# Attention and two expert layers on one core: first scores ahead of first transposes, and an opening spread over three units

## Chip, core and metric

One core of a Trainium2 chip runs the whole program. The metric is device time in microseconds. TensorE multiplies and transposes, VectorE (DVE), ScalarE (ACT) and GpSimd (POOL) do the element work, and SyncE (SP) issues most transfers.

## What is computed

Attention over 2 batches, 8 heads, 768 rows and a head dimension of 64, masked so that a query sees only the keys of its own hash bucket, then a gated layer, then a layer of 8 experts. The change touches only attention.

```python
mask = q_bucket[:, :, :, None] == k_bucket[:, :, None, :]
scores = scale * np.matmul(q, k.transpose(0, 1, 3, 2))
scores = np.where(mask, scores, -1000000000.0)
scores = scores - np.max(scores, axis=-1, keepdims=True)
attn = np.exp(scores)
attn = attn / (np.sum(attn, axis=-1, keepdims=True) + 1e-09)
return np.matmul(attn, v).astype(np.float32)
```

The bucket of a row is made of the signs of six projections. Here the mask is added to the scores by a second product over signed features, so that rows of other buckets fall to a large negative value.

## The kernel before

The program is under a manual schedule: every engine takes its instructions in the order in which the code emits them, and each waits for what it reads and for the tile that it overwrites.

Two heads make a pair, and there are eight pairs. A **unit** is one head and 256 query rows, so a pair has six units and attention has 48. One iteration `u` of the loop at L418 works on several units at once: scores of unit u, the turned probabilities of unit w = u-2, products with the values of x = u-3, and the end of y = u-4.

- `scores(u, t)` (L236): four products into one of two score tiles (`st`), for 128 query rows.
- `rowmax` (L251) on DVE and `expo` (L256) on ACT; `expo` is the last reader of a score tile and also gives the row sums. `masked` (L265) makes two small factors on POOL.
- `recip` (L274) on DVE and `normal` (L278) on POOL: the reciprocal of the sums, then two passes (L282) over the probability tiles of a unit.
- `etrans(w, m)` (L284), m = 0, 1, 2: four transposes into one of three tiles of the pool `ps_t`. `ehigh` (L298) copies the high part out on ACT, `elow` (L302) the low part on DVE; `elow` is the last reader of the tile.
- `pv` (L306): four products of one part with the values, twelve in a unit; `epilogue` (L321) copies out on ACT, and `finish` (L334) adds on POOL.
- A pair's queries and keys are turned ahead of time in six chunks (L346), one in each iteration: four of three transposes (`prep_t`, L154, with a high part on ACT and a low part on DVE) and two of six feature products (`prep_z`, L201). `stack_parts` (L181) and `stack_features` (L195) then copy the parts into the operand tile `p` by transfers from SP, and `load` (L128) fetches the next raw queries, keys and values on SP. `split_v` (L146) splits the values on POOL.

In an iteration TensorE gets scores(u,0), the chunk, etrans(w,1), scores(u,1), pv(x,0), etrans(w,2), pv(x,1), pv(x,2), and at the end etrans(u-1,0), whose copies (`ehigh(w, 0)`, `elow(w, 0)`) come in the next iteration. Weight preparation for the later layers is spread over the iterations by `hook(u, place)`.

The first head has no chunks ahead of it. `stacked` (L375) splits raw queries or keys in place with ACT and DVE, `turned` (L381) transposes them into `p`, and `featured` (L390) makes the mask's rows. L407 to L415 do the keys and the first half of the queries. In iteration 0 (L429 to L433, L454 to L465) the second head's queries, the second half of the first head's queries, the second head's keys and their transfers follow, with the loads of two values; its feature products come in iteration 1. The second pair's first two chunks are at the end of iteration 0 (L493).

Of the kernel before, what the change touches and what calls it, by code (L numbers as in the profile page):

```python
# [8 lines left out]
F32 = mybir.dt.float32  # L9
# [16 lines left out]
class Kernel:  # L26
# [84 lines left out]
    def attention(self, xh, xl, pools, hook):  # L111
        nc = self.nc
        sb, ps_s, ps_t, ps_pv = pools
        NB = self.proj.shape[1]
        NF = self.NF
        S, D = self.S, self.D
        NC = S // 128
# [8 lines left out]
        raw, HL, FT, P, VS, Z = {}, {}, {}, {}, {}, {}  # L126

        def load(i, which="qkv", queue=nc.sync):  # L128
            b, hp = pairs[i]
            for nm in which:  # L130
                src = {"q": self.q, "k": self.k, "v": self.v}[nm]
                if nm == "v":
                    t = sb.tile([128, 2, NC, D], F32, tag="raw", name="raw", bufs=4)
                else:
                    t = sb.tile([128, NC, 2, D], F32, tag="raw", name="raw", bufs=4)
                for j in range(2):
                    queue.dma_start(
                        out=t[:, j] if nm == "v" else t[:, :, j, :],
                        in_=src[b, 2 * hp + j].rearrange("(p c) d -> p c d", c=NC),
                    )  # L140
                raw[i, nm] = t
# [12 lines left out]
        def prep_t(i, nm, half):  # L154
            if half == 0:
                HL[i, nm] = sb.tile([128, 2, S], F32R, tag="hl" + nm, name="hl" + nm, bufs=2 if nm == "q" else 1)
            h, l = (0, 1) if nm == "q" else (1, 0)
            r, hl = raw[i, nm], HL[i, nm]
            pt = ps_t.tile([128, 512], F32, tag="t", name="pt")
            for m in range(3):  # L160
                c = 3 * half + m
                nc.tensor.transpose(pt[:, m * 128:(m + 1) * 128], r[:, c].rearrange("p h d -> p (h d)"), self.ident)
            cols = slice(384 * half, 384 * half + 384)
            scale = float(D) ** -0.5 if nm == "q" else 1.0

            def high():
                nc.scalar.mul(hl[:, h, cols], pt[:, :384], scale)

            def low():
                nc.vector.scalar_tensor_tensor(  # L170
                    hl[:, l, cols], pt[:, :384], scale, f32(hl[:, h, cols]), ALU.mult, ALU.subtract
                )

            return high, low
# [6 lines left out]
        def stack_parts(i, j, which="qk"):  # L181
            if which[0] == "q":
                P[i, j] = sb.tile([128, 4, S], F32R, tag="p", name="p", bufs=2)
            d = slice(64 * j, 64 * j + 64)
            p = P[i, j]
            if "q" in which:
                qs = f32(HL[i, "q"])
                nc.sync.dma_start(out=f32(p[0:64, 0:4:2]), in_=qs[d, 0:1].to_broadcast([64, 2, S]))
                nc.sync.dma_start(out=f32(p[64:128, 0]), in_=qs[d, 1])
            if "k" in which:  # L190
                ks = f32(HL[i, "k"])
                nc.sync.dma_start(out=f32(p[0:64, 1:4:2]), in_=ks[d])
                nc.sync.dma_start(out=f32(p[64:128, 1]), in_=ks[d, 1])
# [42 lines left out]
        def scores(u, t):  # L236
            i, j, g = units[u]
            c = 2 * g + t
            st = ST[u, t] = ps_s.tile([128, 2, 512], F32, tag="s", name="st")
            ql = slice(c * 128, (c + 1) * 128)  # L240
            p = P[i, j]
            for n in range(2):
                kl = slice(n * 384, (n + 1) * 384)
                nc.tensor.matmul(st[:, n, :384], p[:, 0, ql], p[:, 1, kl], start=True, stop=False)  # L244
                nc.tensor.matmul(st[:, n, :384], p[:KP, 2, ql], p[:KP, 3, kl], start=False, stop=True)  # L245
# [38 lines left out]
        def etrans(u, m):  # L284
            pt = ps_t.tile([128, 512], F32, tag="t", name="et")
            for t in range(2):
                for cc in range(2):
                    e = E[u, t].rearrange("p a b -> p (a b)")
                    c = 2 * m + cc
                    nc.tensor.transpose(  # L290
                        pt[:, (2 * cc + t) * 128:(2 * cc + t + 1) * 128],
                        e[:, c * 128:(c + 1) * 128], self.ident,
                    )
            eh = sb.tile([128, 512], F32R, tag="eh", name="eh", bufs=5)
            el = sb.tile([128, 512], F32R, tag="el", name="el", bufs=5)
            ET[u, m] = (eh, el, pt)
# [47 lines left out]
        NU = len(units)  # L344
# [3 lines left out]
        def chunk(n):  # L348

            i, m = divmod(n + 1, per)  # L350
            if i + 1 < len(pairs):
                f, *args = chunks[m]
                return f(i + 1, *args)
            return None

        raw[0, "k"], raw[0, "q"] = (sb.tile([128, NC, 2, D], F32, tag="raw", name="raw", bufs=4) for _ in range(2))
        for j in range(2):
            for nm, src, queue in (("k", self.k, nc.sync), ("q", self.q, nc.scalar)):
                queue.dma_start(
# [15 lines left out]
        def stacked(t, cs):  # L375
            s, r = stacks[t], raw[0, "qk"[t]][:, cs, 0, :]
            scale = 1.0 if t else float(D) ** -0.5
            nc.scalar.mul(s[:, cs, t, :], r, scale)
            nc.vector.scalar_tensor_tensor(s[:, cs, 1 - t, :], r, scale, f32(s[:, cs, t, :]), ALU.mult, ALU.subtract)
# [34 lines left out]
        self.features()  # L414
        load(1, "qk")  # L415

        opening = [[(nm, half) for half in range(2)] for nm in "qk"]
        for u in range(NU + 4):  # L418
            i, r = divmod(u, per)
            w, x, y = u - 2, u - 3, u - 4  # L420
            act, last, tr, out = u < NU, 0 <= u - 1 < NU, 0 <= w < NU, 0 <= x < NU
            if act:
                scores(u, 0)
            if y >= 0:
                epilogue(y)
            prep = chunk(u) if 0 < u < NU else None
            if act:
                rowmax(u, 0)
            if u == 0:  # L429
                for args in opening[0]:  # L430
                    for g in prep_t(0, *args):
                        g()
                stack_parts(0, 1, "q")  # L433
            if last:
                recip(u - 1)
            if tr:
                ehigh(w, 0)
            if last:
                normal(u - 1)
            hook(u, 3)  # L440
            if tr:
                elow(w, 0)
            hook(u, 0)
            if tr:
                etrans(w, 1)
                ehigh(w, 1)
            if act:
                scores(u, 1)
            if tr:
                elow(w, 1)  # L450
            if act:
                rowmax(u, 1)
                masked(u)
            if u == 0:  # L454

                stacked(0, slice(3, NC))
                turned(0, 1)
                featured(0, 1)
                for args in opening[1]:
                    for g in prep_t(0, *args):  # L460
                        g()
                stack_parts(0, 1, "k")
                load(0, "v")
                load(1, "v")
                hook(-1, 1)  # L465
            if u == 1:
                for half in range(2):
                    prep_z(0, half)[1]()
                stack_features(0, 1)
            if out:  # L470
                pv(x, 0)
            if act:
                expo(u, 0)
            if tr:
                etrans(w, 2)
            if out:
                pv(x, 1)
                pv(x, 2)
            if prep:
                prep[0]()  # L480
            hook(u, 2)
            if u in (1, 2):
                split_v(0, u - 1)
            if r >= 4 and i + 1 < len(pairs):
                split_v(i + 1, r - 4)
            if prep:
                prep[1]()
            if tr:
                ehigh(w, 2)
            if y >= 0:  # L490
                finish(y)
            hook(u, 1)
            if u == 0:  # L493
                for n in (-1, 0):
                    for g in chunk(n):
                        g()
            if r == 3 and i + 2 < len(pairs):
                load(i + 2)
            elif r >= 4 and i + 1 < len(pairs):
                stack(i + 1, r - 4)  # L500
            if last:
                etrans(u - 1, 0)
            if act:
                expo(u, 1)
            if tr:
                elow(w, 2)
            hook(u, 4)
# [876 lines left out]
```

## Time and profile before

| | us |
|---|---|
| median of 3 runs | 776.56 (776.48 to 777.78) |
| the profiled execution | 777.34 |
| its span, first to last instruction | 775.5 |
| TensorE busy | 755.2 (97%) |
| DVE, ACT, POOL busy | 494.3, 413.7, 485.4 |

The profiled execution is one run; its span leaves out 1.84 us before and after the instructions. In the rows below a line such as L290 is the line of the kernel that issued the instruction, PE is TensorE's products, PEld its weight loads, and names such as `et<-ident,e` say which tile is written from which. TensorE's busy time is modelled, since products overlap, so the start of one instruction to the start of a later one tells more than busy time.

### The profile page before, as it was taken

How to read it: one execution, taken by the hardware profiler on the slowest of the kernel's cores; microseconds unless marked ns; L12 is line 12 of the kernel's file. 1: busy time of each engine (PE TensorE's matmuls, PEld its weight loads, DVE VectorE, ACT ScalarE, POOL GpSimd, SP SyncE). 2: the span in 40 equal slices, each digit the busy share in tenths (PEclk: the TensorE clock that was granted, in tenths of full speed). 3: DMA queues.
4: the chain of work that ended last, by engine and by line, in shares of the span. 5: the costliest groups of instructions: out<-in, count | busy, mean ns of one | idle time of the engine just before them, and what ended most of it. 6: DMA issues, size and time to landing. Idle time of an engine off the chain costs nothing. (4 is left out here: it accounts for less than half of the span.)

```text
span 775.5 us, 13205 instructions
## 1 busy us (share of the span) xinstructions
PE 755.2 (97%) x4772; PEld 699.0 (90%) x4772; DVE 494.3 (64%) x790; ACT 413.7 (53%) x802; POOL 485.4 (63%) x530
## 2 busy tenths in 40 slices
PE   7999999999999999999999999999999999999996
PEld 5898899999999999999999999999998898899995
DVE  6898889988887755474664645533753755555551
ACT  3798898998988733321221212133443655565651
POOL 2689988888888767264553654644331865565651
PEclk9999999999999999999999999999999999999999
DMA  7864745844451313031111221063361666676620
GB/s 166 193 138 99 180 112 116 177 98 103 102 114 40 109 31 133 1 108 55 55 55 55 69 94 54 2 218 108 95 192 52 206 217 222 223 242 203 212 75 22
DMA packets 65443, 92.06 MB, mean 119 GB/s; under 512 B 28779, under 2 KB 32875, under 8 KB 65376
## 3 DMA queue, kind: packets, MB, share of 16 engines
q1 hardware_dynamic: 61168, 83.45, 38.7%
q0 software_dynamic: 2560, 7.34, 2.5%
q8 instruction: 39, 0.64, 0.3%
q10 hardware_dynamic: 1648, 0.39, 0.2%
q14 instruction: 28, 0.23, 0.1%
HBM read 66.08 MB, written 7.34 MB: 95 GB/s over the span
## 5 line engine op out<-in xcount | busy, mean ns | idle before, releaser
L658 PE MATMUL ab<-xh,w 128*128 128x384 f32 x768 | 204.0, 338 | 0.0
L658 PEld LDWEIGHTS ab<-xh,w 128*128 128x128 f32 x768 | 139.5, 188 | 0.8
L658 PE MATMUL ab<-xl,w 128*128 128x384 f32 x384 | 129.1, 336 | 0.0
L672 POOL TENSOR_TENSOR g<-a,g 128x384 fp32r<-128x384 f32 x48 | 52.4, 1092 | 101.0 <-ACT g L671 94.6
L907 POOL TENSOR_TENSOR w<-raw,w 128x1024 fp32r<-128x1024 f32 x36 | 87.5, 2432 | 37.3 <-ACT w L906 36.2
L254 DVE TENSOR_REDUCE nm<-st 128x1 f32<-128x768 f32 x96 | 91.3, 951 | 21.9 <-PE st L245 17.0
L304 DVE TENSOR_TENSOR el<-et,eh 128x512 fp32r<-128x512 f32 x144 | 96.0, 679 | 11.4 <-ACT eh L300 11.0
L684 PE MATMUL yp<-w,g 128*128 128x512 f32 x432 | 102.9, 390 | 0.0
L282 POOL TENSOR_SCALAR e<-e,s,mc 128x768 f32<-128x768 f32 x96 | 94.8, 995 | 5.2
L290 PE MATMUL et<-ident,e 128*128 128x128 f32 x576 | 91.5, 277 | 6.2 <-POOL e L282 3.7
L684 PEld LDWEIGHTS yp<-w,g 128*128 128x128 f32 x432 | 80.4, 188 | 14.9
L300 ACT CAST eh<-et 128x512 fp32r<-128x512 f32 x144 | 83.1, 587 | 18.6 <-PE et L290 16.3
L260 ACT ACTIVATE e<-st,nm 128x768 f32<-128x768 f32 x96 | 86.8, 904 | 5.2 <-DVE nm L254 2.2
L671 ACT CAST g<-a 128x384 fp32r<-128x384 f32 x48 | 24.7, 515 | 108.9 <-DVE a L670 108.9
L1001 PE MATMUL op<-w,hth 128*128 128x512 f32 x256 | 81.7, 400 | 0.0
L290 PEld LDWEIGHTS et<-ident,e 128*128 128x128 f32 x576 | 65.6, 140 | 16.7 <-POOL e L282 7.9
L951 PE MATMUL hp<-xgh,w 128*128 128x256 f32 x448 | 80.7, 281 | 0.0
L316 PE MATMUL pv<-eh,splv 128*128 128x256 f32 x288 | 76.9, 296 | 0.0
L666 ACT COPY a<-ab 128x384 f32<-128x384 f32 x48 | 22.9, 477 | 97.0 <-PE ab L658 95.5
L244 PE MATMUL st<-p 128*128 128x384 f32 x192 | 73.0, 380 | 0.4 <-ACT e L260 0.3
L907 DVE TENSOR_TENSOR w<-raw,w 128x1024 fp32r<-128x1024 f32 x28 | 63.0, 2251 | 16.1 <-ACT w L906 16.1
L658 PEld LDWEIGHTS ab<-xl,w 128*128 128x128 f32 x384 | 72.3, 188 | 0.8
(193 smaller groups left out, 1551.4 us busy)
## 6 DMA issues: line engine op xcount, KB each, us to landing
raw<-in_moe_w_dram SPq DMA_DIRECT2D x32, 1024.0 KB
p<-hlq SPq DMA_DIRECT2D x15, 384.0 KB
p<-hlk SPq DMA_DIRECT2D x15, 384.0 KB
raw<-in_moe_w_a_dram SPq DMA_DIRECT2D x5, 1024.0 KB
raw<-in_moe_w_b_dram SPq DMA_DIRECT2D x5, 1024.0 KB
raw<-in_moe_w_out_dram SPq DMA_DIRECT2D x5, 1024.0 KB
raw<-in_k_dram SPq DMA_DIRECT2D x16, 192.0 KB
raw<-in_v_dram SPq DMA_DIRECT2D x16, 192.0 KB
```

Of the source, the lines that this page charges most:

```text
L254: nc.vector.tensor_reduce(NM[u][:, t:t + 1], ST[u, t][:, :, :384], axis=AX.XY, op=ALU.max, negate=True)
L260: nc.scalar.activation(e, ST.pop((u, t))[:, :, :384], AF.Exp, bias=NM[u][:, t:t + 1], accum_out=SU[u][:, t:t + 1])
L282: nc.gpsimd.tensor_scalar(E[u, t], E[u, t], r[:, t:t + 1], c[:, t:t + 1], ALU.mult, ALU.add)
L290: nc.tensor.transpose(pt[:, (2 * cc + t) * 128:(2 * cc + t + 1) * 128], e[:, c * 128:(c + 1) * 128], self.ident,)
L300: nc.scalar.copy(eh, pt)
L304: nc.vector.tensor_tensor(el, pt, f32(eh), ALU.subtract)
L316: nc.tensor.matmul(p, w, parts[x][:, cc * 256:(cc + 1) * 256], start=(c == 0 and x == 0), stop=(c == NC - 1 and x == 1),)
L658: nc.tensor.matmul(p[:, :384], w[:, k, fs], x[:, k, cols], start=(k == 0 and n == 0), stop=(k == self.KD - 1 and n == 2),)
L684: nc.tensor.matmul(p, g[:, f, rows], w[:, f], start=(n == 0), stop=(n == 5))
L907: eng.tensor_tensor(l, raw, f32(h), ALU.subtract)
L951: nc.tensor.matmul(p[:, :256], w[:, k, fs], x[:, k], start=(n == 0), stop=(n == 3 * self.KD - 1))
L1001: nc.tensor.matmul(p, h[:, 2 * n + f, rows], w[:, f], start=(n == 0 and f == 0 and m == 0), stop=(n == 3 and f == 1 and m == 2),)
```

## The change

The raw tiles of the first queries and keys are made in the other order. In every iteration the first transposes now follow the scores: `etrans(w, 0)` at the start of iteration u, behind `scores(u, 0)`, in place of `etrans(u - 1, 0)` at the end of the iteration before. In iteration 0 the second half of the query stack is split ahead of the query transposes, the load of the first values follows the query transfers, and `expo(0, 0)` goes ahead of `turned` and `featured`. The second head's key transposes, key transfers and the load of the next values move to iteration 1. The second pair's first two chunks move to the end of iteration 1; its third and fourth are both in iteration 2. `hook(-1, 1)` holds no job. `masked` is not moved.

```diff
-        raw[0, "k"], raw[0, "q"] = (sb.tile([128, NC, 2, D], F32, tag="raw", name="raw", bufs=4) for _ in range(2))
+        raw[0, "q"], raw[0, "k"] = (sb.tile([128, NC, 2, D], F32, tag="raw", name="raw", bufs=4) for _ in range(2))
...
+        OPEN = {1: (), 2: (1, 2)}
...
             if act:
                 scores(u, 0)
+            if tr:
+                etrans(w, 0)
             if y >= 0:
                 epilogue(y)
-            prep = chunk(u) if 0 < u < NU else None
+            preps = [chunk(n) for n in OPEN.get(u, (u,))] if 0 < u < NU else []
+            preps = [prep for prep in preps if prep]
             if act:
                 rowmax(u, 0)
             if u == 0:
+                stacked(0, slice(3, NC))
                 for args in opening[0]:
                     for g in prep_t(0, *args):
                         g()
                 stack_parts(0, 1, "q")
+                load(0, "v")
+            if u == 1:
+                for args in opening[1]:
+                    for g in prep_t(0, *args):
+                        g()
+                stack_parts(0, 1, "k")
+                load(1, "v")
+                hook(-1, 1)
...
             if u == 0:
 
-                stacked(0, slice(3, NC))
+                expo(u, 0)
                 turned(0, 1)
                 featured(0, 1)
-                for args in opening[1]:
-                    for g in prep_t(0, *args):
-                        g()
-                stack_parts(0, 1, "k")
-                load(0, "v")
-                load(1, "v")
-                hook(-1, 1)
...
-            if act:
+            if act and u:
                 expo(u, 0)
...
-            if prep:
+            for prep in preps:
                 prep[0]()
...
-            if prep:
+            for prep in preps:
                 prep[1]()
...
-            if u == 0:
+            if u == 1:
                 for n in (-1, 0):
                     for g in chunk(n):
                         g()
...
-            if last:
-                etrans(u - 1, 0)
```

## Rows read from the trace of the kernel before

**Rows 1.** Busy time by stretch: PE, PEld, DVE, ACT, POOL, clock, DMA share, GB/s.

```profile
98.00:252.00 154.00, 151.45 (x1112) 143.00 (x1110) 134.53 (x221) 138.61 (x298) 134.05 (x225) 1.00 0.50 108
262.00:775.00 513.00, 504.82 (x2998) 467.28 (x2996) 271.50 (x399) 192.35 (x327) 271.95 (x162) 1.00 0.34 114
```

**Rows 2.** Timeline of PE, start and length: first scores of units, and one next instruction.

```profile
44.49 0.41 PE L244 MATMUL st<-p 128*128 128x384 f32 x1
...
131.61 0.42 PE L244 MATMUL st<-p 128*128 128x384 f32 x1
...
132.40 0.49 PE L162 MATMUL pt<-ident,raw 128*128 128x128 f32 x3
...
136.31 0.41 PE L244 MATMUL st<-p 128*128 128x384 f32 x1
...
151.13 0.41 PE L244 MATMUL st<-p 128*128 128x384 f32 x1
...
156.32 0.44 PE L244 MATMUL st<-p 128*128 128x384 f32 x1
...
226.30 0.41 PE L244 MATMUL st<-p 128*128 128x384 f32 x1
```

**Rows 3.** Waits in 29 to 50 (first row) and 50 to 98: total, times, longest.

```profile
PEld et L290 <- POOL e L282: 0.8, 2, 0.5
...
PEld et L290 <- POOL e L282: 3.5, 6, 0.8
...
POOL s L280 <- DVE r L276: 0.6, 1, 0.6
```

**Rows 4.** Waits in 98 to 252 us.

```profile
PEld et L290 <- POOL e L282: 2.6, 8, 0.5
...
PE et L290 <- DVE el L304: 1.4, 3, 0.5
...
POOL s L280 <- DVE r L276: 3.3, 8, 0.6
```

**Rows 5.** Timeline of PE: transposes that wait for POOL (idle time in brackets).

```profile
59.13 0.44 PE L290 MATMUL et<-ident,e 128*128 128x128 f32 x2 [0.34 <-POOL e L282]
```

**Rows 6.** Timelines of PE and ACT: first transposes, and their high copy (two merged).

```profile
131.26 0.60 PE L290 MATMUL et<-ident,e 128*128 128x128 f32 x4
...
132.88 1.13 ACT L300 CAST eh<-et 128x512 fp32r<-128x512 f32 x2
```

**Rows 7.** Timeline of PE in the opening.

```profile
14.56 0.52 PE L385 MATMUL pt<-ident,stack 128*128 128x128 f32 x3 [1.96 <-DVE stack L379]
...
16.35 2.90 PE L162 MATMUL pt<-ident,raw 128*128 128x128 f32 x12
19.29 0.45 PE L244 MATMUL st<-p 128*128 128x384 f32 x1
...
23.32 0.69 PE L213 MATMUL z<-hlk,lz 128*48 128x384 f32 x3
...
28.89 0.41 PE L244 MATMUL st<-p 128*128 128x384 f32 x1
```

**Rows 8.** Timelines of DVE and ACT in the opening.

```profile
11.28 0.96 DVE L254 TENSOR_REDUCE nm<-st 128x1 f32<-128x768 f32 x1 [0.89 <-PE st L245]
...
14.07 0.35 DVE L379 SCALAR_TENSOR_TENSOR stack<-raw,stack 128x192 fp32r<-128x192 f32 x1
...
26.21 1.27 DVE L304 TENSOR_TENSOR el<-et,eh 128x512 fp32r<-128x512 f32 x2
...
18.26 0.89 ACT L260 ACTIVATE e<-st,nm 128x768 f32<-128x768 f32 x1
```

**Rows 9.** Busy time by stretch, as in rows 1, with the clock third from the end.

```profile
15.70:19.10 3.40, 3.40 (x14) 2.70 (x14) 2.21 (x4) 1.72 (x4) 0.00 (x0) 0.50 0.29 59
```

**Rows 10.** SP's issue of the features, and busy time of a stretch behind it.

```profile
24.75 1.75 SPq L199 DMA_DIRECT2D p<-ft  x2
...
26.00:28.00 2.00, 1.62 (x10) 1.00 (x9) 2.00 (x5) 1.97 (x5) 1.84 (x4) 1.00 0.29 58
```

## The prediction

> **What bounds the kernel now.** I read the busy time by stretch first. After 262 us TensorE is busy 504.82 of 513 us and holds nothing of the change, so whatever attention gains or loses ahead of that point moves the end by as much; in 98 to 252 it is busy 151.45 of 154, and what can be won there is the small rest [rows 1]. The spacing of first scores says how much that is. Unit 6 starts at 44.49 and unit 42 at 226.30: 181.81 us, or 30.30 for six units. A unit with three turning transposes and hardly a wait takes 4.70 (131.61 to 136.31), one with feature products 5.19 (151.13 to 156.32); four of the one and two of the other make 29.18 [rows 2]. So 1.12 us is lost per six units, 6.7 in the 36 units.
>
> The waits say on what. TensorE's weight loads wait for POOL's normalised scores at the transposes: 0.8 us in 29 to 50, 3.5 in 50 to 98 [rows 3], 2.6 in 98 to 252, where the matmuls also wait 1.4 for DVE's low part, in three long waits [rows 4]. One such wait closely: the transposes of a tile's second half start at 59.13 after 0.34 of idling for POOL's normalised tile, and the scores of the next unit, which need nothing of it, stand behind them [rows 5]. It is a loop: scores, row maximum, reciprocal, normalise, transposes, next scores.
>
> **The steady part.** The change swaps two neighbours on TensorE: scores(u,0) now go ahead of etrans(w,0). No instruction is added; the transposes stay in line behind the same probability tiles. Three effects.
>
> First, the transposes start the length of the scores later, 0.79 us (131.61 to 132.40, where the next instruction starts [rows 2]). The longest wait for POOL is 0.8 in 50 to 98 and 0.5 after [rows 3, 4], so each single wait fits into it.
>
> Second, scores(u,0), the row maximum behind them and the reciprocal behind that come earlier by the four transposes, 0.35 (131.26 to 131.61 [rows 2, 6]), and by the wait that is gone. POOL waits 3.3 us in eight places for just that reciprocal in 98 to 252 [rows 4].
>
> Third, the high copy of etrans(w,0) on ACT is released later. In an undisturbed unit the transposes end at 131.86 (131.26 and 0.60) and ACT begins that copy at 132.88 [rows 6]. The 1.02 of margin shrinks by 0.8 to 0.2: no cost, but it is the cover to watch. If it goes, the copy waits, and behind it on ACT the second copy, expo(u,0) and the turning copies; DVE's low part waits for the copy, and etrans(w,2) for the tile that the low part frees.
>
> What of the 6.9 of waiting for POOL is won? In 29 to 50 nearly all, 0.7 of 0.8. In 50 to 98 POOL itself waits for the reciprocal once, 0.6 [rows 3]: it is occupied nearly throughout, so it cannot deliver faster. There I take 0.6 for its earlier start and 0.8 of new slack, which can be spent once: 1.4 of 3.5. In 98 to 252 POOL has 3.3 of idling to give; I take 2.0 of 2.6. The 1.4 of waiting for DVE's low part stays: nothing shortens DVE or the ACT copy ahead of it. Steady sum: 4.1 us less. Bounds: 0, if the wait only moves to ACT, and 6.9.
>
> **The opening.** Here three units are rearranged; the old times are in [rows 7, 8]. In unit 0 the split of the query stack is moved ahead of the six query transposes. ACT is idle then, so its multiply is hidden; DVE's 0.35 stands behind the row maximum (11.28 and 0.96): done at 12.5, not 14.4. It holds up the low parts of the queries, the second row maximum and the first SP copies to p by about 1 us, and those have spare time. The turning transposes start at 12.6, not 14.56. The exponential, 0.89 plus its sum, is put ahead of their ACT copy and frees the first score tile at 13.6, not after 19.2. DVE finishes the query half at about 15.4. The key transposes and those of the next pair no longer stand before unit 1: in the old order twelve of them take 2.90 from 16.35, and scores(1,0) start at 19.29. In the new they start at about 14.6.
>
> Unit 1 takes what was removed: six key transposes, ACT's two high and DVE's two low parts, two SP copies of the keys, the load of the second v, the first two turning chunks at its end. With the clock as in the old trace, half granted from 15.70 to 19.10 [rows 9], I get: key transposes done 16.8 (half of 2.90 is 1.45, from 15.5 with some overlap), low parts 17.8 (two ACT copies counted as 0.57 each at most [rows 6], then DVE), scores(1,1) 18.2, the twelve feature products 20.7. In the old trace they end at 24.0 (23.32 and 0.69). DVE's features follow at 21.4, the six transposes and scores(2,0) at 21.4.
>
> Unit 2 has two chunks and the first etrans. Its chain runs through ACT: two turning copies to 22.1, expo(1,1) to 23.1, high copy 23.6, low part 24.3 (a low part is 0.63, half of 1.27 [rows 8]), second transposes 24.7, copy 25.3, expo(2,0) 26.3, which frees the tile of scores(3,0): 26.3 instead of 28.89. That is 2.6 less. At full clock the feature products lose about 1.5 of that and the chain ends near 24.8, but then the transfers are late next. SP's order is kept: query copies, first v, key copies, second v, features. In the old trace the features are issued at 24.75 and packets still run in 26 to 28 [rows 10], at most 3.3 from issue to landing; issued at 21.5 they are there at 24.8, and at full clock, with the second v still in front, at about 25.2. So the bounds are 3.7 less and, if scores(1,0) have to wait for all of the query half (0.8 more) and a second stretch at half clock adds 0.8, 1.0 less. The first v now takes the raw tile of the queries, free at 12.5, and is issued behind the query copies, not after 20: nothing waits for it but POOL's split, which comes later. The two raw tiles made in the other order change addresses and no instruction: nothing.
>
> On the clock: the row shows 0.50 of full speed, the lower of the two levels, after TensorE had stood idle for most of 12.6 to 14.56 [rows 7, 9]. The Trainium skill ("TensorE: Matmul & The Clock Gate", Part 1) says that a throttled clock is the default state and that activity releases it. By that the shorter idle time of the new opening could keep the clock at 2.4 GHz and the opening would give 3.7, not 2.6; the trace has one fall only and cannot say.
>
> **Sum.** The profiled execution took 777.34 (span 775.5 and 1.84 around it), 0.78 above the median of 776.56. 777.34 - 2.6 - 4.1 = 770.6; less 0.78, 769.9 against the median. A measurement of this kernel tells about 0.2%, 1.55 us, from no change.
>
> **The rivals.** *A: the wait moves.* Etrans(w,2) waits for DVE's low part instead, as it does three times now; DVE and ACT gain nothing, steady gain 0. For it: ACT works through every unit with a margin of only 0.2 left. Against: those waits are 1.4 in all. Only the opening stays: 774.0. *B: the opening gives nothing*, because scores(3,0) wait for the features or the rearranged chain on ACT is longer than my hand count: 772.5. *C: the clock stays full* in the opening, so that the twelve products run at the spacing of later ones: 768.8. *D, slower:* the margin on ACT is not 0.2 but missing by 0.25 in each of the 44 steady units, with ACT at its limit so that nothing is caught up: 11.0 more, less 6.7, gives 780.9. It decides once the transposes end more than 1.02 later than now; scores of 0.8 speak against it. *E:* nothing comes of either part, 776.6, for instance when POOL's work fills every unit and the opening is bound by transfers.
>
> **How the numbers follow.** Forecast 0.52, A 0.15, B 0.10, C 0.10, E 0.06, D 0.07. Faster: forecast, B, C and nearly all of A, 0.86; same: E and a rest of A, 0.07; slower: D, 0.07. The range goes from 766.1 (3.7 and 6.8 both won) to 775.2 (A with an opening of 1.3); it leaves out D, E and small ends.
>
> **What would show it.** Right: scores(3,0) at 25 to 27.5; first scores of unit 42 some 6 to 7 earlier than 226.30; TensorE's waits for POOL's tile under 3 in 29 to 252; POOL's waits for the reciprocal smaller. Wrong: ACT waiting at the first high copy in many units; the waits for DVE's low part grown by several us; features landing after 26; a second stretch at half clock.

## The result, and the profile after

The kernel takes **769.25 us** with the change (median of 4 runs, 768.62 to 770.00), against 776.80 for the kernel before in the same comparison (776.48 to 777.78): a ratio of 0.990, with a 95% interval of 0.9885 to 0.9913. The profiled execution took 769.63, its span is 767.8; the span before was 775.5, so 7.7 us are gone from one trace to the other. Lines below the changed ones have numbers that are 4 higher in the kernel after; those ahead of them, such as L244 and L290, keep theirs.

Where did they go? Second scores, scores(u,1), have the same place in the order in both kernels, so their starts can be set against each other. First three of them in the kernel before (units 3, 16 and 46, from the timeline of PE: start, duration, engine, line, operation), then the same three in the kernel after, with the first scores of unit 42 among them.

```profile
31.06 0.42 PE L244 MATMUL st<-p 128*128 128x384 f32 x1
...
98.67 0.42 PE L244 MATMUL st<-p 128*128 128x384 f32 x1
...
248.80 0.42 PE L244 MATMUL st<-p 128*128 128x384 f32 x1
```

```profile
27.79 0.42 PE L244 MATMUL st<-p 128*128 128x384 f32 x1
...
93.55 0.42 PE L244 MATMUL st<-p 128*128 128x384 f32 x1
...
217.61 0.34 PE L244 MATMUL st<-p 128*128 128x384 f32 x1
...
240.43 0.42 PE L244 MATMUL st<-p 128*128 128x384 f32 x1
```

The opening wins 3.27 (31.06 to 27.79) by unit 3. By unit 16 the lead is 5.12, by unit 46 it is 8.37, so the steady part wins 5.10, of which 3.25 lie between units 16 and 46. (A second profile of the same kernel has 8.66 at unit 46, so such leads are good to some 0.3.) From 8.37 to the 7.7 of the spans some 0.7 is lost again behind attention (see the last section). First scores of unit 42 start at 217.61 against 226.30 [rows 2], 8.7 earlier.

To compare the steady part on equal work I took the same 30 units of both kernels, from the second scores of unit 16 to those of unit 46. Busy time of that stretch, before and after (the columns are those of rows 1):

```profile
98.67:248.80 150.13, 147.58 (x1084) 139.38 (x1082) 130.66 (x214) 135.91 (x292) 130.29 (x221) 1.00 0.51 111
...
93.55:240.43 146.88, 144.77 (x1083) 139.05 (x1082) 130.84 (x214) 135.56 (x292) 129.83 (x221) 1.00 0.52 114
```

The same products take 3.25 less, but TensorE's idle time falls by 0.44 only (2.55 to 2.11): the other 2.81 is gone from its modelled busy time, which therefore holds pauses. Groups by line for the transposes, before (busy and mean; behind the second bar the idle time just ahead of them and what ended it):

```profile
L290 PE MATMUL et<-ident,e 128*128 128x128 f32 x363 | 57.0, 276 | 2.5 <-DVE el L304 1.4 <-POOL e L282 0.8
L290 PEld LDWEIGHTS et<-ident,e 128*128 128x128 f32 x361 | 41.3, 140 | 7.9 <-issue 2.8 <-POOL e L282 2.4
```

The same groups after:

```profile
L290 PE MATMUL et<-ident,e 128*128 128x128 f32 x363 | 54.9, 274 | 1.9 <-DVE el L304 1.9
L290 PEld LDWEIGHTS et<-ident,e 128*128 128x128 f32 x361 | 42.7, 141 | 5.8 <-DVE el L304 3.3
```

POOL is gone from the releasers. DVE's low part is now the only one, and in these units it may not have grown: before, 2.8 of the loads' idle time ended in "issue", in seven waits, and now seven waits end in DVE's low part. A single unit shows such a pause. Second scores of units 17 and 18 before, then the same two after:

```profile
103.15 0.42 PE L244 MATMUL st<-p 128*128 128x384 f32 x1
...
107.83 0.42 PE L244 MATMUL st<-p 128*128 128x384 f32 x1
```

```profile
98.03 0.42 PE L244 MATMUL st<-p 128*128 128x384 f32 x1
...
102.51 0.42 PE L244 MATMUL st<-p 128*128 128x384 f32 x1
```

The same 38 products and transposes take 4.68 before and 4.48 after. Neither has a row with idle time, and both count as wholly busy. The unit ahead of it takes 4.48 in the kernel before too (98.67 to 103.15), so 4.48 is such a unit without pauses.

The waits of DVE show the rest of the story, in 98 to 252 us (total, times, longest). Before, with a wait of POOL:

```profile
DVE nm L254 <- PE st L245: 11.3, 21, 1.1
...
DVE el L304 <- ACT eh L300: 5.8, 15, 0.5
...
POOL mk L267 <- DVE nm L254: 2.0, 6, 0.4
```

After, with TensorE's waits in 50 to 98 in the first two rows (the one for POOL is the only one that is left) and POOL's waits for DVE in 98 to 252:

```profile
PEld et L290 <- POOL e L282: 1.7, 4, 0.8
PEld et L290 <- DVE el L304: 1.3, 4, 0.5
...
DVE el L304 <- ACT eh L300: 14.7, 37, 1.0
DVE nm L254 <- PE st L245: 1.1, 3, 0.4
...
POOL mk L267 <- DVE nm L254: 3.4, 8, 0.8
POOL s L280 <- DVE r L276: 1.7, 4, 0.7
```

DVE no longer waits for scores (11.3 to 1.1); it waits for ACT's high copies instead (5.8 to 14.7). POOL waits 1.7 for the reciprocal where it waited 3.3 [rows 4], but 3.4 for the row maxima where it waited 2.0. In 50 to 98, 1.3 of waiting for DVE's low part is new: there a part of the wait only moved. This is what the swap of two neighbours does: scores come earlier, transposes later, and most of the wait goes to engines that have room.

The opening after, from the timeline of PE, with one weight load (in brackets the idle time before, and its releaser):

```profile
14.21 0.34 PE L244 MATMUL st<-p 128*128 128x384 f32 x1
...
15.48 0.42 PE L244 MATMUL st<-p 128*128 128x384 f32 x1
...
18.53 1.08 PE L162 MATMUL pt<-ident,raw 128*128 128x128 f32 x6
...
22.30 0.66 PE L290 MATMUL et<-ident,e 128*128 128x128 f32 x4 [0.90 <-DVE el L304]
...
24.36 0.66 PE L290 MATMUL et<-ident,e 128*128 128x128 f32 x4 [0.70 <-DVE el L304]
24.78 0.42 PE L244 MATMUL st<-p 128*128 128x384 f32 x1
...
25.31 0.19 PEld L245 LDWEIGHTS st<-p 76*128 76x128 f32 x1 [0.37 <-DMA p<-ft]
...
25.34 0.41 PE L245 MATMUL st<-p 76*128 76x384 f32 x1
```

SP's timeline has the issue of the features:

```profile
21.17 1.73 SPq L199 DMA_DIRECT2D p<-ft  x2
```

And the busy time of the stretch of rows 9, with the granted clock third from the end:

```profile
15.70:19.10 3.40, 3.35 (x21) 2.21 (x19) 3.37 (x7) 1.65 (x5) 1.27 (x3) 1.00 0.73 196
```

Scores(3,0) start at 24.78, not 28.89 [rows 7]: 4.11 earlier, but they now stand ahead of four transposes that stood ahead of them, so the 3.27 at scores(3,1) is the fair figure. The twelve feature products are through at 18.5, where the next transposes begin, not at 24. After them TensorE waits 0.90 and 0.70 for DVE's low parts, and inside scores(3,0) the second product starts 0.56 behind the first, where 0.26 is usual after transposes: it needs the features, and its weight load waits for their transfer. The clock is at 2.4 GHz throughout, where it was half granted before [rows 9].

### The profile page after: what moved, and what is told of

It reads as the page before. It is cut to its first block, busy times and chain, and to the rows that moved or that the text cites. A ratio compares the mean times of both kernels' runs of the same rounds, so it can differ in the third digit from the quotient of the medians.

```text
span 767.8 us, 13162 instructions
## 1 busy us (share of the span) xinstructions
PE 749.4 (98%) x4772; PEld 697.0 (91%) x4772; DVE 493.4 (64%) x790; ACT 413.5 (54%) x802; POOL 484.0 (63%) x530
## 5 line engine op out<-in xcount | busy, mean ns | idle before, releaser
L676 POOL TENSOR_TENSOR g<-a,g 128x384 fp32r<-128x384 f32 x48 | 54.6, 1138 | 101.6 <-ACT g L675 95.3
L290 PE MATMUL et<-ident,e 128*128 128x128 f32 x576 | 88.0, 275 | 5.2 <-DVE el L304 4.3
L290 PEld LDWEIGHTS et<-ident,e 128*128 128x128 f32 x576 | 67.9, 141 | 13.3 <-DVE el L304 7.9
L316 PE MATMUL pv<-el,splv 128*128 128x256 f32 x288 | 72.7, 282 | 0.0
```

Source lines behind the costliest of these rows:

```text
L290: nc.tensor.transpose(pt[:, (2 * cc + t) * 128:(2 * cc + t + 1) * 128], e[:, c * 128:(c + 1) * 128], self.ident,)
L316: nc.tensor.matmul(p, w, parts[x][:, cc * 256:(cc + 1) * 256], start=(c == 0 and x == 0), stop=(c == NC - 1 and x == 1),)
```

## The experiments

**The swap alone, with the old opening.**

```diff
-            if last:
-                etrans(u - 1, 0)
...
             if act:
                 scores(u, 0)
+            if tr:
+                etrans(w, 0)
```

> The kernel before with the swap of scores(u,0) and the first transposes alone; its opening is the old one. If the two parts add, the swap is worth the 5.1 us by which the second scores of unit 46 gained on those of unit 3 in the changed kernel's trace (8.37 less 3.27): 771.7, ratio 0.9935, and first scores of unit 3 stay at 28 to 29 us. If the swap pays only because the new opening lets POOL start ahead, it is worth 1 to 2 us: 775 to 776. Weight loads' wait for POOL's tile in 98 to 252 should be under 0.5, from 2.6.

772.02 us (771.12 to 773.79), ratio 0.9937 (0.9924 to 0.9950): 4.9 less than before. TensorE's loads have no wait for POOL's tile left in 98 to 252. Scores(3,0) start at 26.87 in the profiled run (773.79), not at 28 to 29, since they too stand ahead of the transposes; there the features are late, by the timeline of PE:

```profile
26.87 0.44 PE L244 MATMUL st<-p 128*128 128x384 f32 x1
28.80 0.41 PE L245 MATMUL st<-p 76*128 76x384 f32 x1 [1.49 <-DMA p<-ft]
```

and a stretch at half the clock (1.2 GHz, 29.79 to 33.20) follows that wait, so scores(3,1) start at 32.52, later than before. The fall of rows 9 is there as well (16.14 to 19.55).

**The opening alone, with the first transposes at their old place.**

```diff
+            if last:
+                etrans(u - 1, 0)
             if act:
                 expo(u, 1)
...
-            if tr:
-                etrans(w, 0)
             if y >= 0:
                 epilogue(y)
```

> The changed kernel with its first transposes put back behind the products of the iteration before, so that only the opening is new. If the parts add: 3.3 us less than before, 773.5, ratio 0.9958; weight loads wait for POOL's tile as before, 6 to 7 us in all. If the old order eats what the opening wins, as POOL binds up to 98 us whatever the start, the gain is under 1.5: above 775.3. TensorE's granted clock should stay full up to 25 us.

775.64 us (12 runs, 774.80 to 778.28), ratio 0.9988 (0.9978 to 0.9997): 0.9 less by the ratio (0.2 to 1.7 by its interval), 1.3 by the medians, where the prediction's own sum wanted 2.6. Timeline of PE:

```profile
26.79 0.63 PE L290 MATMUL et<-ident,e 128*128 128x128 f32 x4 [0.76 <-DVE hlk L170]
27.18 0.42 PE L244 MATMUL st<-p 128*128 128x384 f32 x1
```

In this order the transposes of unit 1 stand ahead of scores(3,0), and in the new unit 2 they wait for the second chunk's tile, which DVE frees late. The lead at scores(3,1) is 1.70 and grows only to 2.00 by unit 46, and TensorE's loads wait for POOL as before: 2.5 in 98 to 252 [rows 4]. So the two parts alone, 4.9 and 0.9 to 1.3, give 5.8 to 6.2, and together 7.5. The opening wins less without the swap.

**The swap alone, with the features put ahead of the second v on SP.** This was to tell what made the features late.

```diff
                 load(0, "v")
-                load(1, "v")
...
                 stack_features(0, 1)
+                load(1, "v")
```

> The kernel before with the swap alone (as order_only), and besides the second v's load moved behind the transfers of the features. Theory 1 (in order_only the second v's packets are what made the features late, 1.49 at scores(3,0), and that idling brought the second half clock): the wait is gone or under 0.5, the clock does not fall a second time, and the time is 1.5 to 2.5 below order_only's 772.0, so 769.5 to 770.5. Rival (the features are issued at 24.09 whatever stands ahead, since DVE makes them late): the wait stays near 1.5 and the time is 772 within 0.7.

771.96 us (771.61 to 772.74), ratio 0.9932 (0.9918 to 0.9946): the rival. SP is free from 22.1 on and still issues the features at 24.27, as late as in the swap alone (24.09), because DVE makes them so late (timeline of DVE):

```profile
23.57 0.67 DVE L219 TENSOR_SCALAR ft<-z,thr,fac 48x384 fp32r<-48x384 f32 x1 [0.39 <-PE z L213]
```

TensorE's wait for them is 0.73 here and the clock did not fall in the profiled run, yet the time is the same. That run shows the swap by itself best. Its second scores of units 3, 16 and 46:

```profile
30.65 0.42 PE L244 MATMUL st<-p 128*128 128x384 f32 x1
...
96.22 0.42 PE L244 MATMUL st<-p 128*128 128x384 f32 x1
...
243.26 0.42 PE L244 MATMUL st<-p 128*128 128x384 f32 x1
```

Against the kernel before that is 0.41, 2.45 and 5.54 earlier: 0.41 in the opening, where this run also had no fall of the clock, and 5.13 in the steady part, the same 5.1 as with the whole change. The steady gain is the swap's alone. What the fall of the clock costs in the swap alone stays open: the profiled runs differ in it, the medians hardly do.

**The clock in the old opening.** Eighteen transposes of the identity, which nothing reads, go into TensorE's idle time.

```diff
                 stacked(0, slice(3, NC))
+                fill = ps_t.tile([128, 512], F32, tag="t", name="fill")
+                for m in range(14):
+                    nc.tensor.transpose(fill[:, m % 4 * 128:m % 4 * 128 + 128], self.ident, self.ident)
                 turned(0, 1)
+                fill = ps_t.tile([128, 512], F32, tag="t", name="fill")
+                for m in range(4):
+                    nc.tensor.transpose(fill[:, m % 4 * 128:m % 4 * 128 + 128], self.ident, self.ident)
                 featured(0, 1)
```

> The kernel before with 18 transposes that nothing reads put into TensorE's two idle stretches of the opening (14 ahead of the second query half's turning, 4 behind it), to keep the clock at the higher level. If half clock from 15.70 to 19.10 is what the opening of the changed kernel did not have to pay, first scores of unit 3 come 1.0 to 1.5 earlier than 28.89 and the time falls by as much: 775.3 to 775.8, with 1.00 granted throughout. If TensorE was not the limit there, the clock stays full and the time is within 0.4 of before. If the filler delays the turning, slower by up to 0.5.

776.54 us (11 runs), ratio 0.9994 (0.9985 to 1.0003): no difference. The clock is at 1.00 in the stretch of rows 9, but scores(3,0) start at 28.22, only 0.67 earlier than before [rows 7]. The busy time of that stretch:

```profile
15.70:19.10 3.40, 2.85 (x18) 2.03 (x18) 2.31 (x5) 2.40 (x7) 0.00 (x0) 1.00 0.35 72
```

In this trace the fall was worth 0.67, less than the 1.0 to 1.5 expected and too little for the interval to tell from nothing. TensorE has idle time in that stretch at full clock (2.85 busy of 3.40), and in both kernels the last transposes ahead of scores(3,0) wait 0.53 for POOL's tile.

**The same kernel again, and the features ahead of the second v in it.**

```diff
                 stack_parts(0, 1, "k")
-                load(1, "v")
                 hook(-1, 1)
...
                     stack_features(0, 1)
+                load(1, "v")
```

> The changed kernel once more, as the measure for the others: 0.9899 of the time before, 768.6 to 770.0.

> The changed kernel with the load of the second v put behind the transfers of the features instead of ahead of them. In the changed kernel the features are issued at 21.17 and scores(3,0) break off from 24.78 to 25.34, 0.39 of it for them. If that transfer is what is late next, it is issued near 19.7, the break goes and the time falls by 0.3 to 0.5: ratio to before 0.9898. If the chain through ACT binds right behind it, no change: 0.9904. The second v has units of time left either way.

769.44 us, ratio 0.9904 (0.9890 to 0.9918), for the kernel after once more, and 769.25, ratio 0.9898 (0.9884 to 0.9912), with the features first. The features are issued 1.1 earlier (20.08) and the break inside scores(3,0) is gone, but scores(3,1) start at 28.12, against 27.79. Inconclusive for the transfer itself: the opening of that profiled run was 0.47 late from unit 0's second scores on, so at most 0.15 was won. The features are not worth more than that; what binds right behind them takes over.

**How much room.** First the transposes one step further back, behind the head preparation of the unit; then in the middle of the first scores, so with half the room.

```diff
-            if tr:
-                etrans(w, 0)
             if y >= 0:
                 epilogue(y)
...
             preps = [prep for prep in preps if prep]
+            if tr:
+                etrans(w, 0)
```

> The changed kernel with the first transposes put one step further back, behind the turning chunk: 0.33 us more room for POOL in units with transposes, 1.04 in units with feature products. If the margin of ACT's first high copy (0.31 where it was looked at, 126.90 to 127.21) is the cover that the prediction named, it is used up and ACT waits at that copy in most units: slower than the changed kernel by 1 to 4, 770.5 to 773.5. If waits for POOL are the only thing that counts, faster by up to 1.7: 767.7.

```diff
             if act:
-                scores(u, 0)
-            if tr:
-                etrans(w, 0)
+                scores(u, 0, (lambda: etrans(w, 0)) if tr else None)
...
                 nc.tensor.matmul(st[:, n, :384], p[:KP, 2, ql], p[:KP, 3, kl], start=False, stop=True)
+                if n == 0 and between:
+                    between()
```

> The changed kernel with the first transposes in the middle of the first scores, behind two of their four products: half of the room. If it is the room that pays, waits for POOL over 0.4 come back, and the row maximum starts as late as it did: 771 to 773, half way to the order before. If the room hardly matters and what pays is that unit 3 no longer waits behind them, within 0.5 of the changed kernel, 769 to 770.

Both are slower than the change (769.44 and 769.25 in the runs above, none over 770.00): 770.79 us (ratio 0.9921, 0.9908 to 0.9934; 770.17 to 772.57) and 771.95 (0.9938, 0.9923 to 0.9953; 770.82 to 774.77). Further back, TensorE's loads wait nowhere for POOL, but ACT and DVE are later: in four of every six units from 14 to 38 ACT's first high copy starts 0.09 behind the end of its transposes, where the kernel after keeps 0.29 or more in every unit from 14 to 41. So the cover on ACT is used up, as the expectation had it. DVE's wait in 98 to 252:

```profile
DVE el L304 <- ACT eh L300: 17.5, 32, 1.1
```

With half the room the row maxima come late again (in this kernel the lines below the scores are 2 higher):

```profile
DVE el L306 <- ACT eh L302: 7.8, 21, 0.6
DVE nm L256 <- PE st L245: 7.2, 14, 0.8
```

All four transposes stand ahead of the last two products here, so this kernel has half the room and row maxima as late as before in one. DVE waits 7.2 for scores, between the 11.3 of before and the 1.1 of after, and the time stands between them too: from the second scores of unit 3 to those of unit 46 it wins 3.37 of the 5.10. What the room and the earlier scores are worth one by one is not separated.

**POOL made lighter, DVE heavier: the mask factors on DVE.**

```diff
-            nc.gpsimd.tensor_scalar(f, NM[u], BIG / 2, 1.0, ALU.is_lt, ALU.mult)
+            nc.vector.tensor_scalar(f, NM[u], BIG / 2, 1.0, ALU.is_lt, ALU.mult)
...
-            nc.gpsimd.tensor_scalar(c, NM[u], BIG / 2, 1.0 / S, ALU.is_ge, ALU.mult)
+            nc.vector.tensor_scalar(c, NM[u], BIG / 2, 1.0 / S, ALU.is_ge, ALU.mult)
```

> The changed kernel with the two small mask factors of a unit on DVE instead of POOL: POOL has some 0.62 us less in every unit, DVE two small instructions more, some 0.15 to 0.3. If POOL's own work is what still binds in 50 to 98, where it idles nowhere and weight loads wait 1.7 for its tile, that wait goes and the time falls by 1.0 to 2.0: 767.5 to 768.5. If DVE is by now the tighter one (1.3 and 3.3 of waits for its low part in 50 to 98 and 98 to 252), those waits grow by 0.1 to 0.2 per unit and it is slower by 1 to 5.

780.22 us, ratio 1.0033 (1.0021 to 1.0046), 10.8 more than the kernel after. Groups by line in 98 to 252:

```profile
L267 DVE TENSOR_SCALAR mk<-nm 128x2 f32<-128x2 f32 x30 | 10.1, 337 | 3.3 <-POOL e L282 0.5
...
L269 DVE TENSOR_SCALAR mc<-nm 128x2 f32<-128x2 f32 x30 | 4.7, 156 | 0.0
```

And the waits of POOL and of the weight loads there:

```profile
POOL s L280 <- DVE r L276: 27.6, 24, 2.2
...
PEld et L290 <- DVE el L304: 4.6, 11, 0.7
```

Two operations on two columns, 0.49 a unit by these rows, cost 10.8 on the whole. By second scores the lead on the kernel after is lost in two parts: 5.4 by unit 16, where one wait of 1.92 for a turned low part and then a stretch at half the clock (82.75 to 86.16) are among it, and 4.4 in the 30 units to unit 46, 0.15 a unit at full clock. POOL gets idle time and spends it waiting for DVE.

**DVE made lighter: no reciprocal.** (A kernel in which POOL divides instead has no measured time.)

```diff
-            R[u] = small("r")
-            nc.vector.reciprocal(R[u], SU.pop(u))
+            R[u] = SU.pop(u)
```

> The kernel after, with the reciprocal of the row sums left out: the scores are multiplied by the mask factor alone, so the rows are not normalised; DVE has one small instruction less in each unit (154 ns), and POOL's factor no longer waits for one. Theory 1 (after the change DVE's queue, by its low parts, sets what TensorE still waits for): DVE's low parts come 0.15 earlier, TensorE's 3.3 of waiting for them in 98 to 252 falls to 1 to 2, POOL starts its normalising earlier in each unit, and the time falls by 1.5 to 4: 765.3 to 767.8. Rival 1 (ACT's high copy is what DVE waits for, 14.7 in 98 to 252, so that a shorter DVE queue only lengthens that wait): the waits of TensorE stay within 0.5 and the time is 769.3 within 0.7. Rival 2 (TensorE is as good as full): the same time as rival 1, but TensorE's waits fall and its other idle time grows.

769.57 us, ratio 0.9897 (0.9881 to 0.9914): the same time, as rival 1 had it. (POOL's factor is the row sum times the mask factor here, not the mask factor alone as the expectation has it; the instructions are the same.) TensorE's loads wait 3.7 for DVE's low part, against 3.3, so rival 2 is out too. DVE's waits in 98 to 252 (lines 1 lower here):

```profile
DVE el L303 <- ACT eh L299: 16.8, 37, 1.0
```

DVE is busy 2.0 less in that stretch (135.51 against 137.53 by the busy times of the stretch) and waits 2.1 more for ACT's high copies (16.8 against 14.7). So a shorter DVE queue wins nothing after the change: DVE waits that much longer for ACT's copy. A longer one costs, by the experiment before.

## Why the prediction was right, and where its terms were off

The time, 769.25, is 0.65 below the forecast of 769.9, and the mechanism is the one foretold: 7.5 less by the medians, where 2.6 and 4.1 were expected. That it is so close is in part luck. Both terms were too small, 8.37 was won by unit 46 where the sum has 6.7, and some 0.7 was lost again behind attention, where the prediction had the lead go to the end in full. By its steps:

- **First effect, the room for POOL: shown.** TensorE's waits for POOL's tile are gone in 98 to 252 and in 29 to 50, and 1.7 is left in 50 to 98, where 3.5 was [rows 3]. The prediction's mark, under 3 in 29 to 252, holds. The kernels with less and with more room are both slower, though the one with less also has later row maxima.
- **Second effect, the earlier reciprocal: shown.** DVE's waits for scores fell from 11.3 to 1.1, and POOL's for the reciprocal from 3.3 to 1.7 in 98 to 252. In 50 to 98 POOL has no wait left, so it is as good as full there, and the 1.2 won (second scores of units 7 and 16 at 50.89 and 98.67 before, at 46.99 and 93.55 after) agrees with the 1.4 taken for that reason.
- **Third effect, the cover on ACT: held.** In the unit at 126.30 the transposes end at 126.90 and ACT begins their copy at 127.21: 0.31 is left of the 1.02 [rows 6], 0.2 was expected, and no unit from 14 to 41 has less than 0.29.

```profile
126.30 0.60 PE L290 MATMUL et<-ident,e 128*128 128x128 f32 x4
...
127.21 1.13 ACT L300 CAST eh<-et 128x512 fp32r<-128x512 f32 x2
```

- **Steady sum: the term for 98 to 252 was too small.** 0.6 of 0.7 and 1.2 of 1.4 came ahead of it; here 3.25 was measured between units 16 and 46, where 2.0 "of 2.6" was taken. The step that failed is the limit on the gain. The prediction took 4.70 for a unit with hardly a wait, and so 6.7 lost in 36 units, which happened to agree with the 6.9 of waits for POOL's tile. Such a unit takes 4.48 without pauses, in both kernels. With 4.48 the same sum gives 28.30 for six units, 2.0 lost of 30.30 and 12.0 in the 36. Only waits with a row were counted, and 2.81 of the 3.25 won here was inside what the profile calls busy. By the starts in the two traces, 2.6 of the 3.25 is time from the first to the fourth transpose of a tile, summed over the 90 tiles; the rest I do not assign.
- **"The 1.4 of waiting for DVE's low part stays".** In 98 to 252 the record has 1.9 at the products and 3.3 at the loads after, in seven waits each; before, the loads' share stood under "issue", in seven waits as well, two in every six units in both traces. There it stayed, and it was larger than read. In 50 to 98 it did not stay: 1.3 is new. A wait put down to "issue" should have been followed to the tile that the instruction writes.
- **The opening: 2.6 was forecast, 3.27 came by scores(3,1).** The forecast kept the half clock and had scores(3,0) at 26.3; the same text says "the chain ends near 24.8, but then the transfers are late next" for full clock, with the features there at about 25.2. The clock stayed full, scores(3,0) started at 24.78 and their second product, which needs the features, at 25.34. That is rival C's mechanism, but not all of it. The forecast had scores(1,1) at 18.2, behind the low parts of the keys, which they do not read; they started at 15.48, before the 15.70 at which it let the clock fall. So the hand count was 2.7 late there whatever the clock. What the clock gave is not separated: alone in the old opening it wins 0.67, where TensorE had idle time; in the new one TensorE is busy 3.35 of 3.40 in that stretch, so half clock could have cost up to 1.7 (an estimate, half of 3.4), and that was not tried. Nor is it shown that the shorter idle time kept the clock up: the swap alone with the features first has the idle time of the old opening, 1.97 ahead of the query transposes, and 1.00 granted in 15 to 20. (The rule that the prediction cited from the Trainium skill, "TensorE: Matmul & The Clock Gate", Part 1, that activity releases the throttle, agrees with the 1.00 in the row, and it does not tell these two runs apart.) Of the signs of being wrong, features landing after 26 and a second stretch at half clock, neither is there.
- **Not seen at all: that the opening leans on the swap.** The prediction added 2.6 and 4.1 as if each could stand alone. The steady part can (5.1 with and without the new opening). The opening does worse alone: it wins 1.70 by scores(3,1), since the transposes it leaves ahead of scores(3,0) wait for a tile of the second chunk, and the swap alone wins 0.41 there. Together they win 3.27. By unit 46 the difference is smaller: 2.00 and 5.54 alone, 8.37 together.
- **The signs.** Unit 42 came 8.7 earlier, not 6 to 7, and scores(3,0) at 24.78, not 25 to 27.5: both past the good end, for the reasons above.
- **Rivals A, B, D and E** did not happen as such. A is true in a part: what TensorE still waits for is DVE's low part, but outside 50 to 98 that was there before. Of D, the nearest thing is the kernel with the transposes further back, where DVE waits more for ACT: 1.4 slower than the change, not 11.

## What to carry to other kernels

In an in-order queue, look for a waiting instruction with an independent neighbour behind it: swapping the two gave both engines of the loop slack here, without an instruction more, and the slack of the third (ACT, 1.02 to 0.31) was the thing to check first. Compare kernels over the same units of work and not over the same microseconds, and count a wait named "issue" with its neighbours before calling it free. Take the price of a unit without pauses from the shortest unit of its kind, and not from one whose busy time is full. Parts of one change may be worth less alone, so measure them apart before adding them up.

## What was not expected of the hardware

A lower clock need not cost much: in the old opening half the clock for 3.4 us was worth 0.67 in the trace that has it mended, since TensorE had idle time to give. And the same idle time ahead of the query transposes was followed by a fall in one run and by none in another: 1.96 in the kernel before [rows 7], 1.97 in the swap alone with the features first.

Behind attention 0.7 of the lead is lost again. The timelines of POOL, DVE and PE in the kernel after show two engines that hold each other up, and what it costs:

```profile
268.87 1.02 POOL L676 TENSOR_TENSOR g<-a,g 128x384 fp32r<-128x384 f32 x1 [0.64 <-ACT g L675]
...
287.55 2.10 POOL L676 TENSOR_TENSOR g<-a,g 128x384 fp32r<-128x384 f32 x1 [2.36 <-ACT g L675]
...
268.88 2.09 DVE L568 SCALAR_TENSOR_TENSOR v<-raw,v 128x1024 int32<-128x1024 int32 x1
...
287.56 1.23 DVE L568 SCALAR_TENSOR_TENSOR v<-raw,v 128x1024 int32<-128x1024 int32 x1
...
289.71 3.24 PE L688 MATMUL yp<-w,g 128*128 128x512 f32 x13 [0.34 <-POOL g L676]
```

Twice the same pair starts within 0.01 us. The first time POOL takes its usual 1.02 and DVE 2.09 instead of 1.23; the second time DVE takes 1.23 and POOL 2.10. The sum of the durations is 3.11 and 3.33, and each time one of the two pays. The Trainium skill ("SBUF — State Buffer", SBUF: two separate sides) says that DVE, with two inputs in SBUF, and a GpSimd instruction that reads SBUF take the same pair of ports as an exclusive lock, for the whole instruction; the rows agree. At 287.55 it hit POOL's, and TensorE waited 0.34 for it. The kernel with the opening alone has the same 0.34, at 296.12, and loses 0.7 of its lead behind unit 46; the swap alone with the features first has none in that product, and loses 0.1. So what is won ahead of this point can be lost in part by where two engines happen to meet; the other 0.3 or so of the 0.7 is in no single row.
